# Rewriting the issue order of the last stage: TensorE's sequence written out, chunks of 2, 2, 4, 4, 4 and 2 tiles

## The chip, the cores and the metric

The kernel runs on one core of a Trainium2 chip. The time is the device time of one execution in microseconds (us). Three runs of the kernel before took 962.36, 962.38 and 963.45 us; their median is 962.38. About 0.2% (1.9 us) is what a measurement of this kernel can tell from no change.

## The reference, cut to what matters

Three layers follow each other. Attention through a small memory gives `x` (2304 tokens x 512). A mixture of eight experts sends each token to its best two. A last layer with a cosine gate gives the output:

```python
for e in range(E):                       # 8 experts, 512 -> 1024 -> 512
    for k in range(2):
        mask = top2[:, k] == e
        h = np.maximum(x[mask] @ w1[e], 0.0)
        out[mask] += top2_w[mask, k, None] * (h @ w2[e])
# last layer, on the experts' result
h = x @ w_in                             # 512 -> 2048
g = h * np.cos(h)
return (g @ w_out).astype(np.float32)    # 2048 -> 512
```

The change touches the seam between the last expert and the last layer, and the last layer itself.

## The kernel before, in words

Tokens are handled as 18 tiles of 128. Numbers that go through a matmul are split into two 16-bit parts, so each product is three matmuls: high by high, high by low, low by high.

**Experts.** Each expert has five second-layer tiles (`NST = 5`, capacity 640 rows). The first layer runs in two parts, over two of the tiles and then over the other three, in eight blocks each (`l1`, and `l1_out` on ScalarE and VectorE); the second layer runs tile by tile (`l2`, `l2_out`). `l2_out` scales on ScalarE and stores 128 rows to `yd` in memory. If an expert has more rows than 640, the loop `overflow` (L919) takes the rest; in these runs it has nothing to do, but its branch still joins all engines. Every matmul of the experts is tied to the one before by `chain("P", ...)`, which fixes TensorE's order.

**Last layer.** It works in chunks of tiles. `comb(t)` gathers a tile's two expert rows per token from `yd` (two indirect DMAs on POOL's queue), weights and adds them, finds a power-of-two scale in a chain of small VectorE instructions, splits the sum, and issues a transposing DMA into `x2T` on SP's queue. One small TensorE transpose (`pb`) and a ScalarE copy (`bct`) spread the scale over the columns. `m1(j, f)` computes block f of 16 of the first product for chunk j: 12 matmuls into one of four PSUM banks, four VectorE instructions (two of which read the bank, the second after a sine on ScalarE), a copy on ScalarE and a subtraction on POOL. Results lie in `gT`, in buffers that raw expert weights and the experts' hidden values used before. `m2_(t)` computes tile t's output: 48 matmuls, a scaled copy on ScalarE, a store.

**What sets the order.** Everything is entered in a list with a due time: `at(t, fn, ...)`. `issue()` sorts the list, and the due time becomes a priority; a scheduler then lays out each engine's queue from the priorities and its own estimate of when each instruction is ready. Only `chain` fixes an order. In the last layer before, nothing is chained, so the scheduler mixes first and second products on TensorE as it sees fit. Due times count from `X[e]`, the start of expert e, and `m0`, the end of the last expert. `put_weights` and `put_chunk` place loading, scaling and splitting of weights in free places (`slot`) on ScalarE and VectorE during the experts. In each engine, instructions run in queue order.

Of the kernel before, what the change touches and what calls it, by code (L numbers as in the profile page):

```python
# [60 lines left out]
def fused_kernel(ctx, tc, phiT, qT, kv, wgn, noise, w1, w2, wi, wo, out):  # L61
# [19 lines left out]
    def at(t, fn, *a, lead=None):  # L81
        line.append((t, len(line), fn, a, LEAD.get(fn.__name__, 0.0) if lead is None else lead))
# [18 lines left out]
    def l2k(shape, dt, name):  # L101
        return lp.tile(shape, dt, tag="l", name=name)
# [709 lines left out]
    def mt(shape, dt, name, bufs=2):  # L812
        return pools["mp"].tile(shape, dt, tag=name, name=name, bufs=bufs)
# [153 lines left out]

    ib = sm([P, NT], F32, "ib")
    x2T, bct = {}, {}
    chunks = [(0, 2), (2, 6), (6, 10), (10, 14), (14, 18)]  # L970
    ch_of = {t: j for j, (a, b) in enumerate(chunks) for t in range(a, b)}

    def comb(t):

        ys = []
        for k in range(2):
            y = l2k([P, DM], F32, f"y{k}")
            rows = min(YROWS, Y0 + (E - 1) * CAP + (t + 1) * P)
            G.indirect_dma_start(out=y, out_offset=None, in_=yd[0:rows],  # L979
                                 in_offset=bass.IndirectOffsetOnAxis(ap=sidx[:, t, k:k + 1], axis=0))  # L980
            ys.append(y)
        yield
        j = ch_of[t]
        o = (t - chunks[j][0]) * P
        if o == 0:
            n = (chunks[j][1] - chunks[j][0]) * P
            x2T[j] = mt([P, 8, n], F16, "x2T")
            bct[j] = mt([P, n], F32, "bct")
        y0, y1 = ys
        V.tensor_scalar(y0, y0, cw[:, t, 0:1], None, op0=OP.mult)  # L990
        V.scalar_tensor_tensor(y1, y1, cw[:, t, 1:2], y0, op0=OP.mult, op1=OP.add)  # L991
        mx = mt([P, 4], F32, "cmx")
        tmp = mt([P, 1], I32, "cmt")
        V.tensor_reduce(mx[:, 0:1], y1, axis=AX.X, op=OP.max, apply_absolute_value=True)
        pow2_scale(mx[:, 1:2], mx[:, 0:1], tmp)
        pow2_inv(ib[:, t:t + 1], mx[:, 1:2])
        V.tensor_scalar(mx[:, 2:3], ib[:, t:t + 1], 1.0 / (2.0 * math.pi), None, op0=OP.mult)
        hl = l2k([P, 2, DM], F16, "chl")
        A.activation(hl[:, 0], y1, AF.Copy, scale=mx[:, 1:2])
        V.scalar_tensor_tensor(hl[:, 1], y1, mx[:, 1:2], hl[:, 0], op0=OP.mult, op1=OP.subtract)  # L1000
        SP.dma_start_transpose(out=x2T[j][:, :, o:o + P], in_=hl.rearrange("p w d -> p (w d)"))
        yield
# [33 lines left out]
    def m1(j, f):  # L1036
        n = (chunks[j][1] - chunks[j][0]) * P
        if f % 8 == 0:
            gT[j, f // 8] = [hs("gT", int(2 * (f // 8) + w + j % 2 > 1), [P, 8, n], F16) for w in range(2)]
        ghi, glo = gT[j, f // 8]  # L1040
        x = x2T[j]
        c = f // 2
        w = win[c // 4][:, c % 4]
        fs = slice((f % 2) * P, (f % 2) * P + P)
        ph = bank_h()
        for k in range(4):
            T.matmul(ph[:, :n], lhsT=w[:, 0, k, fs], rhs=x[:, k, :], start=(k == 0), stop=False)  # L1047
            T.matmul(ph[:, :n], lhsT=w[:, 0, k, fs], rhs=x[:, 4 + k, :], start=False, stop=False)  # L1048
            T.matmul(ph[:, :n], lhsT=w[:, 1, k, fs], rhs=x[:, k, :], start=False, stop=(k == 3))  # L1049
        y = mt([P, 512], F32, "ty", 3)  # L1050
        t = mt([P, 512], F32, "tt", 3)
        V.scalar_tensor_tensor(y[:, :n], ph[:, :n], wis[:, 2 * E + c:2 * E + c + 1], bct[j], op0=OP.mult, op1=OP.mult)  # L1052
        V.tensor_scalar(t[:, :n], y[:, :n], 0.25, MAGIC, op0=OP.add, op1=OP.add)  # L1053
        V.scalar_tensor_tensor(t[:, :n], t[:, :n], MAGIC, y[:, :n], op0=OP.subtract, op1=OP.subtract)  # L1054
        A.activation(t[:, :n], t[:, :n], AF.Sin, bias=hp, scale=-2.0 * math.pi)  # L1055
        V.scalar_tensor_tensor(y[:, :n], ph[:, :n], fac[:, c:c + 1], t[:, :n], op0=OP.mult, op1=OP.mult)  # L1056
        A.activation(ghi[:, f % 8, :], y[:, :n], AF.Copy)  # L1057
        G.tensor_tensor(glo[:, f % 8, :], y[:, :n], ghi[:, f % 8, :], op=OP.subtract)  # L1058

    def m2_(t):  # L1060
        j = ch_of[t]
        cs = slice((t - chunks[j][0]) * P, (t - chunks[j][0] + 1) * P)
        po = bank_y()
        for f in range(16):
            ghi, glo = gT[j, f // 8]
            w = wout[f // 8][:, (f // 2) % 4]
            T.matmul(po, lhsT=ghi[:, f % 8, cs], rhs=w[:, 0, f % 2, :], start=(f == 0), stop=False)  # L1067
            T.matmul(po, lhsT=ghi[:, f % 8, cs], rhs=w[:, 1, f % 2, :], start=False, stop=False)  # L1068
            T.matmul(po, lhsT=glo[:, f % 8, cs], rhs=w[:, 0, f % 2, :], start=False, stop=(f == 15))  # L1069
        o = l2k([P, DM], F32, "o")  # L1070
# [48 lines left out]
    for e in range(E):  # L1119
        if e:  # L1120
            X.append(x)
            for f in range(8):
                x = put_l1(x, e, 0, f)
            if 0 < e < E - 1:
                at(x + 0.1, gather_x, e + 1, 0, False)
                for c in range(CA):
                    at(x + 4.0 + 0.5 * c, turn_x, e + 1, 0, c)
        for f in range(8):
            x = put_l1(x, e, 1, f)
        if e == 0:  # L1130
# [74 lines left out]
    x = X[7] + 8 * sum(d1)
    for t in range(6):
        y = x + d2 * (min(t, NST - 1) + 1) + 3.0 + (2.0 if t == 5 else 0.0)
        whole(y, comb, t)
    nj = len(chunks)
    x = m0  # L1210
    dm = lambda j: 16 * (1.4 if chunks[j][1] - chunks[j][0] == 2 else 2.64)

    def put_m1(j):
        nonlocal x
        for f in range(16):
            at(x + dm(j) / 16 * f, m1, j, f)
        x += dm(j)

    put_m1(0)
    for j in range(1, nj + 1):  # L1220
        if j < nj:
            put_m1(j)
        u0 = x
        for t in range(*chunks[j - 1]):
            at(x, m2_, t)
            x += 10.4
        if j + 1 < nj:
            per = (x - u0 - 2.0) / 4
            for k, t in enumerate(range(*chunks[j + 1])):
                y = u0 + per * k - 14.0  # L1230
                whole(y, comb, t)
    issue()


# [34 lines left out]
```

## Time and profile before

| | |
|---|---|
| median of three runs | 962.38 us |
| the profiled execution | 961.89 us |
| its span, first to last instruction | 960.1 us |
| mean granted TensorE clock | 0.964 |
| PE busy | 889.6 us (93%) |
| PEld (weight loads) busy | 496.9 us (52%) |
| DVE (VectorE) busy | 586.1 us (61%) |
| ACT (ScalarE) busy | 450.6 us (47%) |
| POOL (GpSimd) busy | 233.8 us (24%) |

A busy share is an average over stages with different limits. A wait is idle time of an engine just before an instruction, put down to what ended it. In the page's slices one digit stands for 24 us, in tenths busy. The last expert starts at about 504 us and the last layer fills the rest.

### The profile page before, as it was taken

What the parts mean: (1) busy time and instruction counts of PE and PEld (TensorE: products, weight loads), DVE (VectorE), ACT (ScalarE), POOL (GpSimd) and SP (SyncE); (2) the same over time, 40 slices, a digit from 0 to 9 for tenths busy, and PEclk for the clock granted to TensorE, in tenths of its full rate; (3) what the DMA queues carried; (4) which work ended last, traced back from release to release, by engine and by line L of the source; (5) the groups of instructions that cost most, each with busy time, mean ns of one, the idle gap of its engine ahead of it and who ended that gap; (6) DMA issues with size and microseconds to landing.
All of it is one profiled execution on the core that took longest, in us unless ns stands there. A gap on an engine that the chain in (4) does not pass through costs nothing. (4 is left out here: it accounts for less than half of the span.)

```text
span 960.1 us, 13569 instructions
## 1 busy us (share of the span) xinstructions
PE 889.6 (93%) x5124; PEld 496.9 (52%) x5124; DVE 586.1 (61%) x1290; ACT 450.6 (47%) x776; POOL 233.8 (24%) x228
## 2 busy tenths in 40 slices
PE   5988179999999999999999989599999999999998
PEld 3756055564747565655646456244444444444443
DVE  4799781375756567665855159599994695285000
ACT  3575603566666767666765125144552253143000
POOL 1354831111011102020100024344453243043000
PEclk9897679999999999999999989799999999999999
DMA  9962219768696879696780442522104102100000
GB/s 355 399 250 76 78 54 271 223 203 292 218 294 214 270 236 310 243 267 248 230 307 35 141 156 77 132 56 67 23 1 121 45 12 79 32 1 12 23 22 34
DMA packets 108244, 146.51 MB, mean 153 GB/s; under 512 B 65808, under 2 KB 66448, under 8 KB 106128
## 3 DMA queue, kind: packets, MB, share of 16 engines
q1 hardware_dynamic: 89536, 103.56, 34.4%
q0 software_dynamic: 6080, 19.93, 6.9%
q10 hardware_dynamic: 12560, 22.13, 6.3%
q8 instruction: 41, 0.67, 0.3%
q14 instruction: 27, 0.22, 0.1%
HBM read 95.26 MB, written 35.13 MB: 136 GB/s over the span
## 5 line engine op out<-in xcount | busy, mean ns | idle before, releaser
L244 PE MATMUL h<-x,w 128*128 128x384 f16 (+1 forms) x1440 | 201.2, 301 | 2.1 <-DVEq L924 2.1
L244 PEld LDWEIGHTS <-w 128*128 128x128 f16 x1440 | 140.9, 99 | 58.6 <-issue 2.8
L1058 POOL TENSOR_TENSOR gT<-ty,gT 128x512 f16<-128x512 f32 (+1 forms) x80 | 95.1, 1190 | 169.8 <-ACT gT L1057 169.8
L1047 PE MATMUL h<-x2T,win 128*128 128x512 f16 (+1 forms) x320 | 116.2, 363 | 8.7 <-DMA x2T<-chl 7.1
L907 PE MATMUL y<-w,hT 128*128 128x512 f16 x320 | 121.3, 379 | 0.0
L906 PE MATMUL y<-w,hT 128*128 128x512 f16 x320 | 121.3, 379 | 0.0
L905 PE MATMUL y<-w,hT 128*128 128x512 f16 x320 | 121.2, 379 | 0.0
L1048 PE MATMUL h<-x2T,win 128*128 128x512 f16 (+1 forms) x320 | 116.1, 363 | 0.0
L1049 PE MATMUL h<-x2T,win 128*128 128x512 f16 (+1 forms) x320 | 115.9, 362 | 0.0
L1067 PE MATMUL y<-wout,gT 128*128 128x512 f16 x288 | 108.8, 379 | 0.2 <-ACT gT L1057 0.2
L1068 PE MATMUL y<-wout,gT 128*128 128x512 f16 x288 | 108.8, 379 | 0.0
L1069 PE MATMUL y<-wout,gT 128*128 128x512 f16 x288 | 108.8, 379 | 0.0
L244 DVE SCALAR_TENSOR_TENSOR hT<-h,hT 128x384 f16<-128x384 f32 (+1 forms) x128 | 61.8, 488 | 72.7 <-ACT hT L244 71.2
L244 ACT ACTIVATE hT<-h 128x384 f16<-128x384 f32 (+1 forms) x128 | 55.8, 436 | 100.7 <-PE h L244 69.2
L244 DVE SCALAR_TENSOR_TENSOR w<-raw,wsc,w 128x1024 f16<-128x1024 f32 x56 | 71.2, 1282 | 26.2 <-ACT w L244 25.8
L1055 ACT ACTIVATE tt<-tt,hp 128x512 f32<-128x512 f32 (+1 forms) x80 | 54.3, 678 | 67.4 <-DVE tt L1054 61.5
L1052 DVE SCALAR_TENSOR_TENSOR ty<-h,wis,bct 128x512 f32<-128x512 f32 (+1 forms) x80 | 55.2, 690 | 45.9 <-PE h L1049 45.3
L1057 ACT ACTIVATE gT<-ty 128x512 f16<-128x512 f32 (+1 forms) x80 | 46.8, 587 | 69.3 <-DVE ty L1056 69.3
L844 POOL DMA_INDIRECT xg<-xd,idxB x24 | 25.8, 1076 | 216.3 <-DMA x<-xg 200.1
L244 ACT ACTIVATE w<-raw,wsc 128x1024 f16<-128x1024 f32 x56 | 62.8, 1139 | 3.8 <-ACT o L244 3.0
L979 POOL DMA_INDIRECT y<-yd,sidx x36 | 36.1, 1002 | 111.5 <-DMA yd<-o 89.6
L244 ACT ACTIVATE junk<-raw 128x1024 bf16<-128x1024 f32 x56 | 58.9, 1052 | 5.1 <-ACT o L244 4.7
(264 smaller groups left out, 1220.3 us busy)
## 6 DMA issues: line engine op xcount, KB each, us to landing
raw<-in_w SPq DMA_DIRECT2D x32, 1024.0 KB, 9.0
yd<-o ACTq DMA_DIRECT2D x40, 256.0 KB, 4.8
kvt<-in_kv SPq DMA_DIRECT2D x9, 1024.0 KB, 9.8
cvt<-in_wi SPq DMA_DIRECT2D x8, 1024.0 KB, 8.2
wst<-cvt SPq DMA_DIRECT2D x16, 512.0 KB, 3.7
cvt<-in_wo SPq DMA_DIRECT2D x8, 1024.0 KB, 6.2
yd<-zero ACTq DMA_DIRECT2D x13, 512.0 KB
xd<-hl SPq DMA_DIRECT2D x18, 256.0 KB, 2.6
```

Source lines behind the costliest of these rows:

```text
L244: last[key] = fn(*a, **kw)
L905: ins = [T.matmul(py, lhsT=hi[:, f, cs], rhs=w[:, 0, ws], start=(f == 0), stop=False), T.matmul(py, lhsT=hi[:, f, cs], rhs=w[:, 1, ws], st ...
L906: T.matmul(py, lhsT=hi[:, f, cs], rhs=w[:, 1, ws], start=False, stop=False),
L907: T.matmul(py, lhsT=lo[:, f, cs], rhs=w[:, 0, ws], start=False, stop=(f == 7))]
L1047: T.matmul(ph[:, :n], lhsT=w[:, 0, k, fs], rhs=x[:, k, :], start=(k == 0), stop=False)
L1048: T.matmul(ph[:, :n], lhsT=w[:, 0, k, fs], rhs=x[:, 4 + k, :], start=False, stop=False)
L1049: T.matmul(ph[:, :n], lhsT=w[:, 1, k, fs], rhs=x[:, k, :], start=False, stop=(k == 3))
L1052: V.scalar_tensor_tensor(y[:, :n], ph[:, :n], wis[:, 2 * E + c:2 * E + c + 1], bct[j], op0=OP.mult, op1=OP.mult)
L1058: G.tensor_tensor(glo[:, f % 8, :], y[:, :n], ghi[:, f % 8, :], op=OP.subtract)
L1067: T.matmul(po, lhsT=ghi[:, f % 8, cs], rhs=w[:, 0, f % 2, :], start=(f == 0), stop=False)
L1068: T.matmul(po, lhsT=ghi[:, f % 8, cs], rhs=w[:, 1, f % 2, :], start=False, stop=False)
L1069: T.matmul(po, lhsT=glo[:, f % 8, cs], rhs=w[:, 0, f % 2, :], start=False, stop=(f == 15))
```

## The change

Chunks become (2, 2, 4, 4, 4, 2) tiles instead of (2, 4, 4, 4, 4). Every matmul of the last layer and every `pb` transpose is tied into `chain("P", ...)`, so that TensorE runs them in the order of their due times. The last expert runs its first part's two second-layer tiles before its second part, and the first four blocks of chunk 0 before its last second-layer tile. From chunk 2 on, second products of one chunk stand between groups of the next chunk's first products. `comb` loses its steps: its first multiply goes to ScalarE, the output scale `osc` is computed there instead of in `m2_`, the scale buffers become four, and the `pb` transpose becomes a function of its own, `c_bct`, with its own due time. The due times of the overflow loop, the pools, the table load, the output weights and the last expert's second weights move.

```diff
-    chunks = [(0, 2), (2, 6), (6, 10), (10, 14), (14, 18)]
+    chunks = [(0, 2), (2, 4), (4, 8), (8, 12), (12, 16), (16, 18)]
...
-        V.tensor_scalar(y0, y0, cw[:, t, 0:1], None, op0=OP.mult)
+        A.activation(y0, y0, AF.Copy, scale=cw[:, t, 0:1])
...
-        mx = mt([P, 4], F32, "cmx")
+        mx = mt([P, 4], F32, "cmx", 4)
...
+        V.tensor_tensor(osc[:, t:t + 1], ib[:, t:t + 1], ik, op=OP.mult)
...
+    def c_bct(t):
+        j, o = c_place(t)
         pb = mbank("pb")
-        T.transpose(pb[:, :P], mx[:, 2:3].to_broadcast([P, P]), ident)
-        A.activation(bct[j][:, o:o + P], pb[:, :P], AF.Copy)
-        yield
+        chain("P", T.transpose, pb[:, :P], cm.pop(t)[:, 2:3].to_broadcast([P, P]), ident)
+        A.activation(bct[j][:, o], pb[:, :P], AF.Copy)
...
-            T.matmul(ph[:, :n], lhsT=w[:, 0, k, fs], rhs=x[:, k, :], start=(k == 0), stop=False)
+            chain("P", T.matmul, ph[:, :n], lhsT=w[:, 0, k, fs], rhs=x[:, k, :], start=(k == 0), stop=False)
...
-            T.matmul(po, lhsT=ghi[:, f % 8, cs], rhs=w[:, 0, f % 2, :], start=(f == 0), stop=False)
+            chain("P", T.matmul, po, lhsT=ghi[:, f % 8, cs], rhs=w[:, 0, f % 2, :], start=(f == 0), stop=False)
...
+        if e == E - 1:
+            for c in range(CA):
+                x = put_l2(x, e, c)
         for f in range(8):
             x = put_l1(x, e, 1, f)
+        if e == E - 1:
+            break
...
+    def put_comb(t, t0, t1):
+        at(t0, comb, t)
+        at(t1, c_bct, t)
+
+    y = [ends[-8 - CA + t] for t in range(2)]
+    put_l2_ = lambda c: put_l2(x, E - 1, c)
+    x = put_l2_(2)
+    x = put_l2_(3)
+    for t in range(2):
+        put_comb(t, y[t] + 3.0, x - 2.0 + t)
+    put_m1(0, range(0, 4))
+    x = put_l2_(4)
     m0 = x
+    put_m1(0, range(4, 16))
+    put_m2(0)
+    put_comb(2, m0 + 3.0, x)
+    put_m2(1)
+    put_comb(3, m0 + 6.0, x - 1.0)
+    put_m1(1, range(16))
+    put_m2(2)
+    for t in range(4, 8):
+        put_comb(t, m0 + 9.0 + 9.0 * (t - 4), x + (0.0 if t < 7 else 9.0))
+    put_m2(3)
+    put_m1(2, range(16))
+    for j, first, u in ((2, 2, 24.0), (3, 0, 58.0), (4, 2, 40.0)):
+        n = chunks[j + 1][1] - chunks[j + 1][0]
+        u0, u1 = x - u, x + first * 10.36
+        for k, t in enumerate(range(*chunks[j + 1])):
+            put_comb(t, u0 + (u1 - u0 - 16.0) / n * k, u1 - 0.2 * n + 0.1 * k)
+        for k in range(4):
+            if k >= first:
+                q = 16 // (4 - first)
+                put_m1(j + 1, range(q * (k - first), q * (k - first + 1)))
+            put_m2(chunks[j][0] + k)
+    for t in range(*chunks[5]):
+        put_m2(t)
...
-    OV, LP, PRE = 22.0, 34.0, 36.0
+    OV, LP, PRE = 13.0, 16.0, 30.0
+    x = X[E - 2]
+    put_weights(2 * E - 1, (x + 12.0, x + 15.0), x + 27.0, 0.0)
...
-        put_chunk(c, X[1] + 2.0 + 19.3 * c)
+        put_chunk(c, X[1] + 2.0 + 18.5 * c)
...
-    at(X[7] + 37.0, load_wout, 0)
-    at(m0 + 0.5, load_wout, 1)
+    at(X[7] + 45.0, load_wout, 0)
+    at(m0 + 4.0, load_wout, 1)
```

`put_m1(j, fs)` places the blocks `fs` of chunk j at 1.31 us (two tiles) or 2.59 us (four), `put_m2(t)` a second product at 10.36 us.

## Rows read from the trace of the kernel before

**Rows 1.** The page's slices: PE's busy tenths in 40 slices of 24 us.
```profile
PE   5988179999999999999999989599999999999998
```
**Rows 2.** PE's waits from 480 us: who, for what: us in total, times, longest.
```profile
PE h L1047 <- DMA x2T<-chl: 7.1, 2, 4.6
PE pb L1004 <- DVE osc L1071: 5.6, 1, 5.6
PE pb L1004 <- ACT bct L1005: 2.2, 1, 2.2
PE h L244 <- DVEq L924: 2.1, 1, 2.1
```
**Rows 3.** Stretches: length, busy us of PE, PEld, DVE, ACT, POOL, clock, DMA.
```profile
560.00:570.00 10.00, 6.73 (x42) 5.11 (x43) 2.92 (x9) 1.40 (x5) 1.89 (x2) 0.66 0.95 308
...
566.40:598.80 32.40, 32.33 (x237) 23.39 (x236) 29.51 (x80) 15.26 (x35) 12.38 (x17) 0.98 0.31 98
```
**Rows 4.** PE in order of time: start, us, instruction, idle time before it.
```profile
503.63 0.27 PE L244 MATMUL h<-x,w 128*128 128x256 f16 x1
...
558.23 0.27 PE L1004 MATMUL pb<-ident,cmx 128*128 128x128 f32 x1
560.71 0.34 PE L1004 MATMUL pb<-ident,cmx 128*128 128x128 f32 x1 [2.20 <-ACT bct L1005]
...
569.42 0.27 PE L1049 MATMUL h<-x2T,win 128*128 128x256 f16 x1
...
571.28 0.27 PE L1048 MATMUL h<-x2T,win 128*128 128x256 f16 x1
...
831.45 0.38 PE L1047 MATMUL h<-x2T,win 128*128 128x512 f16 x1
...
841.81 0.38 PE L1067 MATMUL y<-wout,gT 128*128 128x512 f16 x1
```
**Rows 5.** ACT in order of time.
```profile
560.38 0.28 ACT L1005 ACTIVATE bct<-pb 128x128 f32<-128x128 f32 x1 [0.41 <-ACT o L244]
561.08 0.28 ACT L1005 ACTIVATE bct<-pb 128x128 f32<-128x128 f32 x1 [0.43 <-PE pb L1004]
...
567.76 0.51 ACT L1055 ACTIVATE tt<-tt,hp 128x256 f32<-128x256 f32 x1 [6.40 <-DVE tt L1054]
...
738.46 0.27 ACT L1005 ACTIVATE bct<-pb 128x128 f32<-128x128 f32 x1
...
945.62 0.69 ACT L1072 ACTIVATE o<-y,osc 128x512 f32<-128x512 f32 x1 [9.67 <-PE y L1069]
...
955.98 0.69 ACT L1072 ACTIVATE o<-y,osc 128x512 f32<-128x512 f32 x1 [9.67 <-PE y L1069]
```
**Rows 6.** DVE's groups by shape, 566 to 876 us: busy, mean ns, idle before.
```profile
L1056 DVE SCALAR_TENSOR_TENSOR ty<-h,fac,tt 128x256 f32<-128x256 f32 x16 | 7.6, 475 | 0.8 <-ACT tt L1055 0.8
L1052 DVE SCALAR_TENSOR_TENSOR ty<-h,wis,bct 128x256 f32<-128x256 f32 x16 | 7.6, 474 | 7.0 <-PE h L1049 7.0
L1054 DVE SCALAR_TENSOR_TENSOR tt<-tt,ty 128x256 f32<-128x256 f32 x16 | 7.4, 460 | 0.1
L1053 DVE TENSOR_SCALAR tt<-ty 128x256 f32<-128x256 f32 x16 | 6.2, 388 | 0.2
```
**Rows 7.** DVE in order of time, in a run of 512-column blocks.
```profile
683.37 0.75 DVE L1056 SCALAR_TENSOR_TENSOR ty<-h,fac,tt 128x512 f32<-128x512 f32 x1 [0.19 <-ACT tt L1055]
...
686.03 0.75 DVE L1056 SCALAR_TENSOR_TENSOR ty<-h,fac,tt 128x512 f32<-128x512 f32 x1 [0.19 <-ACT tt L1055]
```
**Rows 8.** DVE in order of time: tile 0's combine, and a lone L1053.
```profile
545.93 0.75 DVE L991 SCALAR_TENSOR_TENSOR y<-y,cw,y 128x512 f32<-128x512 f32 x1 [0.99 <-DMA y<-yd,sidx]
...
548.76 0.75 DVE L1000 SCALAR_TENSOR_TENSOR chl<-y,cmx,chl 128x512 f16<-128x512 f32 x1 [0.34 <-ACT chl L999]
...
566.97 0.29 DVE L1053 TENSOR_SCALAR tt<-ty 128x256 f32<-128x256 f32 x1
```
**Rows 9.** The gathers of the last layer, 540 to 830 us.
```profile
DMA to landing us min/median/max: 3.3/4.3/7.3
```

More of the change, by code (lines that the diff above doesn't have):

```diff
@@ L969, in fused_kernel, with c_place @@
     x2T, bct = {}, {}
-    chunks = [(0, 2), (2, 6), (6, 10), (10, 14), (14, 18)]
+    chunks = [(0, 2), (2, 4), (4, 8), (8, 12), (12, 16), (16, 18)]
     ch_of = {t: j for j, (a, b) in enumerate(chunks) for t in range(a, b)}
+    cm = {}
+    def c_place(t):
+        j = ch_of[t]
+        return j, slice((t - chunks[j][0]) * P, (t - chunks[j][0] + 1) * P)
     def comb(t):
[L975 to L978, printed above, removed]
+        rows = min(YROWS, Y0 + (E - 1) * CAP + (t + 1) * P)
+        y0, y1 = (l2k([P, DM], F32, f"y{k}") for k in range(2))
+        for k, y in enumerate((y0, y1)):
             G.indirect_dma_start(out=y, out_offset=None, in_=yd[0:rows],
                                  in_offset=bass.IndirectOffsetOnAxis(ap=sidx[:, t, k:k + 1], axis=0))
-            ys.append(y)
-        yield
-        j = ch_of[t]
-        o = (t - chunks[j][0]) * P
-        if o == 0:
+        j, o = c_place(t)
+        if t == chunks[j][0]:
             n = (chunks[j][1] - chunks[j][0]) * P
@@ L988, in comb @@
             bct[j] = mt([P, n], F32, "bct")
-        y0, y1 = ys
-        V.tensor_scalar(y0, y0, cw[:, t, 0:1], None, op0=OP.mult)
+        A.activation(y0, y0, AF.Copy, scale=cw[:, t, 0:1])
         V.scalar_tensor_tensor(y1, y1, cw[:, t, 1:2], y0, op0=OP.mult, op1=OP.add)
-        mx = mt([P, 4], F32, "cmx")
+        mx = mt([P, 4], F32, "cmx", 4)
         tmp = mt([P, 1], I32, "cmt")
@@ L1000, in comb @@
         V.scalar_tensor_tensor(hl[:, 1], y1, mx[:, 1:2], hl[:, 0], op0=OP.mult, op1=OP.subtract)
-        SP.dma_start_transpose(out=x2T[j][:, :, o:o + P], in_=hl.rearrange("p w d -> p (w d)"))
-        yield
+        SP.dma_start_transpose(out=x2T[j][:, :, o], in_=hl.rearrange("p w d -> p (w d)"))
+        cm[t] = mx
+    def c_bct(t):
+        j, o = c_place(t)
         pb = mbank("pb")
-        T.transpose(pb[:, :P], mx[:, 2:3].to_broadcast([P, P]), ident)
-        A.activation(bct[j][:, o:o + P], pb[:, :P], AF.Copy)
-        yield
+        chain("P", T.transpose, pb[:, :P], cm.pop(t)[:, 2:3].to_broadcast([P, P]), ident)
+        A.activation(bct[j][:, o], pb[:, :P], AF.Copy)
     win, wout = [], []
@@ L1038, in m1 @@
         if f % 8 == 0:
-            gT[j, f // 8] = [hs("gT", int(2 * (f // 8) + w + j % 2 > 1), [P, 8, n], F16) for w in range(2)]
-        ghi, glo = gT[j, f // 8]
+            gT[j, f // 8] = [hs("gT", int(j % 2 == 0 or 2 * (f // 8) + w == 3), [P, 8, n], F16) for w in range(2)]
         x = x2T[j]
@@ L1046, in m1 @@
         for k in range(4):
-            T.matmul(ph[:, :n], lhsT=w[:, 0, k, fs], rhs=x[:, k, :], start=(k == 0), stop=False)
[L1048 to L1058, printed above, removed]
+            chain("P", T.matmul, ph[:, :n], lhsT=w[:, 0, k, fs], rhs=x[:, k, :], start=(k == 0), stop=False)
+            chain("P", T.matmul, ph[:, :n], lhsT=w[:, 0, k, fs], rhs=x[:, 4 + k, :], start=False, stop=False)
+            chain("P", T.matmul, ph[:, :n], lhsT=w[:, 1, k, fs], rhs=x[:, k, :], start=False, stop=(k == 3))
+        y = mt([P, 512], F32, "ty", 3)[:, :n]
+        t = mt([P, 512], F32, "tt", 3)[:, :n]
+        ghi, glo = gT[j, f // 8]
+        V.scalar_tensor_tensor(y, ph[:, :n], wis[:, 2 * E + c:2 * E + c + 1], bct[j], op0=OP.mult, op1=OP.mult)
+        V.tensor_scalar(t, y, 0.25, MAGIC, op0=OP.add, op1=OP.add)
+        V.scalar_tensor_tensor(t, t, MAGIC, y, op0=OP.subtract, op1=OP.subtract)
+        A.activation(t, t, AF.Sin, bias=hp, scale=-2.0 * math.pi)
+        V.scalar_tensor_tensor(y, ph[:, :n], fac[:, c:c + 1], t, op0=OP.mult, op1=OP.mult)
+        A.activation(ghi[:, f % 8, :], y, AF.Copy)
+        G.tensor_tensor(glo[:, f % 8, :], y, ghi[:, f % 8, :], op=OP.subtract)
     def m2_(t):
-        j = ch_of[t]
-        cs = slice((t - chunks[j][0]) * P, (t - chunks[j][0] + 1) * P)
+        j, cs = c_place(t)
         po = bank_y()
@@ L1066, in m2_ @@
             w = wout[f // 8][:, (f // 2) % 4]
-            T.matmul(po, lhsT=ghi[:, f % 8, cs], rhs=w[:, 0, f % 2, :], start=(f == 0), stop=False)
-            T.matmul(po, lhsT=ghi[:, f % 8, cs], rhs=w[:, 1, f % 2, :], start=False, stop=False)
-            T.matmul(po, lhsT=glo[:, f % 8, cs], rhs=w[:, 0, f % 2, :], start=False, stop=(f == 15))
+            chain("P", T.matmul, po, lhsT=ghi[:, f % 8, cs], rhs=w[:, 0, f % 2, :], start=(f == 0), stop=False)
+            chain("P", T.matmul, po, lhsT=ghi[:, f % 8, cs], rhs=w[:, 1, f % 2, :], start=False, stop=False)
+            chain("P", T.matmul, po, lhsT=glo[:, f % 8, cs], rhs=w[:, 0, f % 2, :], start=False, stop=(f == 15))
         o = l2k([P, DM], F32, "o")
-        V.tensor_tensor(osc[:, t:t + 1], ib[:, t:t + 1], ik, op=OP.mult)
         A.activation(o, po, AF.Copy, scale=osc[:, t:t + 1])
@@ L1103, in put_l1 @@
         ends.append(x)
-        if part or f % 2:
+        if part or f % 4:
             free.append(x + 0.05)
@@ L1137, in fused_kernel, with put_m1, put_m2 @@
             x = put_l2(x, e, c)
-    m0 = x
+    def put_m1(j, fs):
+        nonlocal x
+        n = chunks[j][1] - chunks[j][0]
+        d = 1.31 if n == 2 else 2.59
+        for f in fs:
+            at(x, m1, j, f)
+            x += d
+    def put_m2(t):
+        nonlocal x
+        at(x, m2_, t)
+        x += 10.36
+    def put_comb(t, t0, t1):
[9 more added lines that the diff above has]
+    x = put_l2_(4)
+    m0 = x
+    put_m1(0, range(4, 16))
[21 more added lines that the diff above has]
+        put_m2(t)
     def next_table():
@@ L1192, in fused_kernel @@
         put_weights(2 * e, (x - 6.0, x - 3.0), x + 11.5, 0.0)
-        put_weights(2 * e + 1, (x + 15.0, x + 18.0), x + 30.0, 0.0)
+        if e < E - 1:
+            put_weights(2 * e + 1, (x + 12.0, x + 15.0), x + 30.0, 0.0)
     bg(slots(), X[1] + 8.0, (0, 6, 12, 18))
@@ L1200, in fused_kernel @@
     at(X[7] + 0.3, load_win, 1)
-    at(m0 - 1.0, factors)
+    at(X[7] + 17.0, factors)
     at(X[7] + PRE, next_table)
-    at(X[7] + 37.0, load_wout, 0)
-    at(m0 + 0.5, load_wout, 1)
[L1205 to L1231, printed above, removed]
+    at(X[7] + 45.0, load_wout, 0)
+    at(m0 + 4.0, load_wout, 1)
     issue()
```

## The prediction

> **What bounds the kernel now.** I read the page's slices first. PE is at nine tenths or more in nearly every slice from the fifth on, except in a hole in slices 23 to 25, where the last expert gives way to the last stage [rows 1]. So outside that hole time can come only from fewer matmuls, and the change removes none. Second, PE's own waits from 480 us on: 7.1 us for a transposed tile, 5.6 us for VectorE's scale of a combined tile, 2.2 us for ScalarE to empty the bank of the small transposes (the pb matmuls), 2.1 us at the branch of the overflow loop; behind these four there is little [rows 2]. Third, the stretches: the granted clock is 0.66 from 560 to 570 us, so the matmuls behind such a hole run partly at the lower level, and from 566.4 to 598.8 us VectorE is busy 29.5 of 32.4 us while PE loses nothing [rows 3]. There PE alternates between first and second products: the second products fill the time in which VectorE is behind.
>
> **How much is at stake.** The last expert's first matmul starts at 503.63 us and the last output copy, which follows PE's end directly, at 955.98 [rows 4, 5]: 452.35 us. The floor of the new order, with the same matmuls:
> - last expert, with the branch: 558.23 - 503.63 = 54.6 [rows 4].
> - first products: 17 matmuls of 256 columns from 569.42 to 571.28, 0.1094 each, so a chunk of two tiles (16 blocks f of 12) costs 21.0; 48 of 512 columns from 831.45 to 841.81, 10.36, so a chunk of four costs 41.44 [rows 4]. Three of each: 187.3. (Trading a chunk of four for two of two adds 0.6.)
> - second products: 10.36 a tile by the distance of the last two output copies [rows 5], 18 tiles: 186.5.
> - 18 pb transposes. Their rows show 0.27 for one, which is pipelined; I take 0.11, that of a 256-column matmul: 2.0.
>
> Sum 430.4, so 22.0 us of holes, slow clock and small waits lie in before's last stage. The branch is not among them: it moves to another place but still joins all engines, and stays at 2.1.
>
> **What the fixed order removes.** With two second-layer tiles of the last expert done early, tile 1's rows are complete at about 23 us after the expert's start (10.5 + 2 x 5.2 + 2.1), and the first products begin at about 49. From the row that starts VectorE's combine to its end takes 3.6 us [rows 8] and a gather 3.3 to 7.3 us to land [rows 9]; even with a store and a transpose of like length that is under 26. So the transfer wait at 563 goes. The one at 619 goes too: tiles 2 and 3 now have at least 36 us of matmuls behind the last expert (12 blocks and two second products), tiles 4 to 7 some 78. I count all 22.0 as removed.
>
> **What it adds, first: pb transposes back to back.** They now stand in PE's order in groups of 2, 1, 1, 3, 1, 4, 4 and 2, and use one PSUM bank. Each later one of a group waits until ScalarE has copied the one before. By the pair in the trace: pb at 560.71, its copy at 561.08 for 0.28, and a copy that ended at 560.66 let the next pb start at 560.71: 0.37 + 0.28 + 0.05 = 0.70 a turn, 0.6 over its own 0.11 [rows 4, 5]. All five groups stand right behind a finished output tile, whose copy (0.69) is ahead on ScalarE; the row at 738.46 shows a bct copy starting without idle time behind such work [rows 5]. So the first turn costs 1.0. Two groups of four 2 x (1.0 + 0.6 + 0.6), one of three 1.6, two pairs 2.0: 8.0 us. Before, PE ran other matmuls there. Low end: the copy goes ahead of the output tile, 10 x 0.6 = 6.0. High end: the output's DMA issue goes first as well, the 0.41 that stands in the row at 560.38, five times: 10.0.
>
> **Second: narrow chunks with nothing between their blocks.** A block f needs four VectorE instructions. Their means at 256 columns are 0.474, 0.388, 0.460 and 0.475 [rows 6]; less about 0.075 by which dense rows overlap, 1.50 a block, against PE's 1.31. High end: the whole stretch of rows 3, 80 VectorE instructions, some 16 blocks and two combines, gives (32.4 - 2 x 2.7)/16 = 1.69. Low end: no slower than PE. A combine keeps VectorE for 1.5 (its two instructions of 0.75 alone) to 3.2 us (from 545.93 to 549.51 less 0.34 idle [rows 8]); I take 2.7, nearer the whole, as the small instructions between cost time too and other blocks fill only part of their gaps. The change moves its first multiply to ScalarE, which is left out here. PE may be four banks ahead: 4 x 1.31, less the block's own 1.31 and its unhurried chain to the second read of the bank, 0.48 + 0.79 (566.97 to 567.76) + 0.51 + 0.03 + 0.48 = 2.3 [rows 5, 8]: 1.64 us of slack.
> - Chunk 0, blocks 4 to 15 (0 to 3 are covered by the last second-layer tile): 12 x 1.50 + 1.5 combines x 2.7 = 22.05 against 15.75 + 1.64: 4.65 us.
> - Chunk 1: 16 x 1.50 + one combine 2.7 = 26.7 against 21.0 + 1.64: 4.05 us. Tile 6 waits for tile 2's pb (four scale buffers), tile 7 for tile 3's, so one of them falls in here.
> - Chunk 5 is cut in halves by a second product: 8 x 1.50 = 12.0 against 10.5 + 1.64: nothing.
> - At 512 columns VectorE's period in steady state is 686.03 - 683.37 = 2.66, of which 0.19 is idle [rows 7], against PE's 2.59 with four times that as lead. Over 16 blocks it falls behind by 1.1, plus two combines, and catches up in the second products: nothing.
>
> Sum 8.7.
>
> **Costed at nothing.** The last expert's second weights are due earlier in the written plan: their last piece at 6.5 us before the expert's start instead of 15.6 after it, needed at 10.5 after; the first weights' last piece comes at 2.5 before, read from 1.2 after. ScalarE and VectorE do the same work there, and PE has no wait from that part [rows 2]; if the cover went, each late piece would cost 1 to 2 us. On SP's queue both loads of the output weights start later; the second has 16.9 us from its due time to its first use, more than twice the slowest gather [rows 9]. The table load lands among the last expert's relus, where PE is four banks ahead. The early stores wait for nothing new. Scales moved from the output to the combine stay on VectorE.
>
> **Sum.** -22.0 + 8.0 + 8.7 = -5.3 us. The profiled execution took 961.89 us, 0.49 below the median of 962.38; carried over to the median: 957.1 us.
>
> **Rivals.**
> - *The order is as free as it was meant*: bct copies go first (6.0) and VectorE keeps up with 1.31. -22.0 + 6.0 = -16.0: 946.4 us. For it: part of the stretch's 29.5 us was combines, which now fall into second products. Against it: 1.50 is a mean of all sixteen blocks.
> - *VectorE is the bound of the narrow chunks*, and PE, whose order is fixed, has nothing to put in between. At 1.7 a block and 3.2 a combine: chunk 0 20.4 + 4.8 - 17.4 = 7.8; chunk 1 27.2 + 3.2 - 22.6 = 7.8; chunk 5 2 x (13.6 - 12.1) = 2.9 (rounded). With 8.0 for the pb turns: +4.5, 966.9 us. It decides from 1.63 a block on, where these stalls reach 14.0. For it: the high end above, and L1053's mean of 0.388 against 0.29 for a lone one [rows 6, 8], beside POOL's subtractions. Against it: that stretch also had more combines.
>   The Trainium skill (page "SBUF — State Buffer", section "Who interferes with whom") says that a VectorE instruction with two SBUF inputs, or in a two-port mode, and a GpSimd instruction that reads SBUF shut each other out for a whole instruction; by that rule the narrow blocks, which bring a subtraction every 1.31 us, fare as in this rival. L1053's 0.1 us of excess agrees in sign, and is far less than a whole subtraction.
> - *Late gathers*: VectorE works in order; if a gather in chunk 0 lands after 7.3 instead of 3.3 us [rows 9], because the second load of weights runs beside it, blocks behind the combine wait 4.0 longer: -1.3, 961.1 us.
> - *The order isn't what it says*: PE's order would still alternate first and second products inside a chunk, and nothing would change. The links are written instruction by instruction, so this is small and counted with the third.
>
> **How the numbers follow.** Forecast 0.42, free order 0.20, VectorE-bound 0.23, late gathers 0.15. 0.2% of 962 is 1.9 us, about what a measurement of this kernel tells from no change. Faster: nearly all of the forecast and the free order, and a little of the third, 0.62. Same: most of the third, 0.14. Slower: VectorE-bound and its neighbours, 0.24. Range: from 947, the free order, to 968, just past the VectorE-bound case. The forecast's own range, from the ends of the pb and VectorE terms short of the rivals, is 952 to 961.
>
> **What would show it.** In the changed profile: no PE wait on a transposed tile; five places with PE waits on ACT bct of 1.0 and 0.6, in all 6 to 10; PE waits in chunks 0 and 1, 4 to 5 in each, on VectorE's second read of the bank (L1056 of before); clock 1.0 from 560 to 625. It is wrong if PE waits on a gather or a scale again, if the wait at the branch grows, or if the narrow chunks run through at 1.31 a block.

## The result: slower, and the profile after

| kernel | median us (runs) | ratio to before, 95% | last stage us |
|---|---|---|---|
| before | 962.4 (959.3 to 963.5, 4) | 1 | 452.3 |
| changed | 976.4 (973.6 to 977.6, 4) | 1.0147 [1.0115, 1.0179] | 465.5 |
| changed, PE's order free (e1) | 943.5 (942.3 to 944.9, 4) | 0.9802 [0.9778, 0.9827] | 433.2 |

Each ratio is to runs of the kernel before taken beside it. The forecast was 957.1 us, faster, and the range ended at 968. "Last stage" is, here and below, the time from the last expert's first matmul to PE's end in the profiled execution, the stretch that the prediction summed up (452.35 to the output copy, floor 430.4). In the changed kernel it runs from 504.13 to 969.67 us: 13.2 us longer than before, 35.1 over the floor.

The page's slices of the changed kernel, PE and the granted clock. Counted from 0, as the prediction does, PE's old hole in slices 23 to 25 [rows 1] has become shallower, and slices 28 and 32 have new dents:

```profile
PE   5988179999999999999999989799799989999998
...
PEclk8988579999999999999999999999999999999999
```

PE's waits in its last stage (from 500 us):

```profile
PE h L244 <- DVE ty L1061: 17.2, 13, 3.8
PE pb L244 <- ACT bct L1010: 6.0, 10, 0.8
PE y L907 <- issue: 2.1, 1, 2.1
PE h L244 <- DVE ib L158: 1.7, 2, 1.2
```

The waits for a transposed tile and for a combine's scale [rows 2] are gone. In their place stand the ten pb turns and thirteen waits for VectorE's second read of a bank (L1061, which is L1056 of before; two more are put down to L158, the instruction right behind an L1061). Where these are, by stretches (length, busy us of PE, PEld, DVE, ACT, POOL, clock, DMA): blocks 4 to 15 of chunk 0, chunk 1, the sixteen blocks of chunk 2, and for comparison four blocks of chunk 4:

```profile
565.10:584.10 19.00, 16.39 (x146) 14.08 (x145) 17.12 (x44) 9.79 (x21) 9.41 (x12) 1.00 0.51 172
605.10:635.00 29.90, 23.38 (x195) 19.67 (x194) 25.90 (x73) 15.04 (x33) 11.32 (x14) 0.94 0.27 55
657.80:710.90 53.10, 45.53 (x194) 19.50 (x192) 48.85 (x93) 23.42 (x36) 23.49 (x19) 0.94 0.23 55
...
822.40:832.80 10.40, 10.40 (x50) 4.71 (x49) 6.60 (x11) 3.39 (x5) 1.50 (x2) 1.00 0.07 26
```

At the floor's rates these stretches take 15.75, 21.0 and 41.44 us. So chunk 0 loses 3.2, chunk 1 8.8 and chunk 2 11.7 us; chunk 3 loses 1.0 and 1.5 in its two halves, chunk 5 0.2. With 8.2 for the pb turns that is 34.6 of the 35.1.

A group of four pb transposes in PE's timeline (start, us, instruction, idle before). The next first product starts 2.70 us after the first pb, where four pb on their own would take 0.44, at the 0.11 from the lone pb at 594.58 to the matmul behind it at 594.69:

```profile
731.65 0.27 PE L244 MATMUL pb<-ident,cmx 128*128 128x128 f32 x1
732.76 0.32 PE L244 MATMUL pb<-ident,cmx 128*128 128x128 f32 x1 [0.84 <-ACT bct L1010]
733.45 0.32 PE L244 MATMUL pb<-ident,cmx 128*128 128x128 f32 x1 [0.37 <-ACT bct L1010]
734.14 0.32 PE L244 MATMUL pb<-ident,cmx 128*128 128x128 f32 x1 [0.37 <-ACT bct L1010]
734.35 1.02 PE L244 MATMUL h<-x2T,win 128*128 128x512 f16 x4
```

VectorE's groups in chunk 2 (first four lines) and in chunk 4 (last line): busy, mean ns of one, idle before. Four combines lie inside chunk 2's run (x4), and L1059 takes half as long again as in chunk 4:

```profile
L1059 DVE SCALAR_TENSOR_TENSOR tt<-tt,ty 128x512 f32<-128x512 f32 x14 | 14.1, 1008 | 0.0
...
L1061 DVE SCALAR_TENSOR_TENSOR ty<-h,fac,tt 128x512 f32<-128x512 f32 x13 | 9.6, 735 | 0.0
...
L1002 DVE SCALAR_TENSOR_TENSOR chl<-y,cmx,chl 128x512 f16<-128x512 f32 x4 | 4.5, 1131 | 0.0
...
L999 DVE TENSOR_TENSOR osc<-ib,ik 128x1 f32<-128x1 f32 x4 | 1.7, 413 | 0.0
...
L1059 DVE SCALAR_TENSOR_TENSOR tt<-tt,ty 128x512 f32<-128x512 f32 x10 | 6.9, 690 | 0.2
```

### The profile page after: what moved, and what is told of

The parts are those of the page before. It is cut to its first block, busy times and chain, and to the rows that moved or that the text cites. A ratio compares the mean times of both kernels' runs of the same rounds, so it can differ in the third digit from the quotient of the medians.

```text
span 973.8 us, 14080 instructions
## 1 busy us (share of the span) xinstructions
PE 896.3 (92%) x5316; PEld 515.9 (53%) x5316; DVE 590.9 (61%) x1336; ACT 468.8 (48%) x826; POOL 235.2 (24%) x244
## 5 line engine op out<-in xcount | busy, mean ns | idle before, releaser
L244 PE MATMUL h<-x2T,win 128*128 128x256 f16 (+1 forms) x1152 | 196.9, 331 | 19.2 <-DVE ty L1061 17.2
L244 PE MATMUL y<-wout,gT 128*128 128x512 f16 x864 | 188.7, 379 | 0.0
L244 PEld LDWEIGHTS <-win 128*128 128x128 f16 x1152 | 114.2, 99 | 99.9 <-issue 27.4
L1063 POOL TENSOR_TENSOR gT<-ty,gT 128x256 f16<-128x256 f32 (+1 forms) x96 | 99.0, 1036 | 264.4 <-ACT gT L1062 264.3
L244 PEld LDWEIGHTS <-gT 128*128 128x128 f16 x864 | 84.5, 98 | 101.2 <-POOL gT L1063 0.7
L1057 DVE SCALAR_TENSOR_TENSOR ty<-h,wis,bct 128x256 f32<-128x256 f32 (+1 forms) x96 | 58.4, 610 | 114.9 <-PE h L244 112.5
L1060 ACT ACTIVATE tt<-tt,hp 128x256 f32<-128x256 f32 (+1 forms) x96 | 58.9, 614 | 79.7 <-DVE tt L1059 69.2
L1062 ACT ACTIVATE gT<-ty 128x256 f16<-128x256 f32 (+1 forms) x96 | 49.9, 521 | 70.6 <-DVE ty L1061 70.1
L1061 DVE SCALAR_TENSOR_TENSOR ty<-h,fac,tt 128x256 f32<-128x256 f32 (+1 forms) x96 | 58.4, 608 | 7.7 <-ACT tt L1060 7.7
L1059 DVE SCALAR_TENSOR_TENSOR tt<-tt,ty 128x256 f32<-128x256 f32 (+1 forms) x96 | 60.8, 634 | 0.7
```

Source lines behind the costliest of these rows:

```text
L244: last[key] = fn(*a, **kw)
L1057: V.scalar_tensor_tensor(y, ph[:, :n], wis[:, 2 * E + c:2 * E + c + 1], bct[j], op0=OP.mult, op1=OP.mult)
L1059: V.scalar_tensor_tensor(t, t, MAGIC, y, op0=OP.subtract, op1=OP.subtract)
L1060: A.activation(t, t, AF.Sin, bias=hp, scale=-2.0 * math.pi)
L1061: V.scalar_tensor_tensor(y, ph[:, :n], fac[:, c:c + 1], t, op0=OP.mult, op1=OP.mult)
L1062: A.activation(ghi[:, f % 8, :], y, AF.Copy)
```

## The experiments

The planner sorts PE's matmuls when the kernel is built, by its own estimates and the due times; on the chip PE always works in order. "Free" below means sorted by the planner, "fixed" written out.

**e1: PE's order free.** `chain("P", ...)` taken off the last stage's products and pb:

```diff
-            chain("P", T.matmul, ph[:, :n], lhsT=w[:, 0, k, fs], rhs=x[:, k, :], start=(k == 0), stop=False)
+            T.matmul(ph[:, :n], lhsT=w[:, 0, k, fs], rhs=x[:, k, :], start=(k == 0), stop=False)
```

> The changed kernel with the last layer's matmuls and pb transposes not tied to each other, so the scheduler orders TensorE as before the change; chunks, early tiles, due times and combine stay. Theory A (the fixed order leaves TensorE nothing to put in while VectorE is behind): the 26 us of waits in chunks 0 to 3 and the 8 us of pb turns are mostly filled again, and the early tiles still save the hole at the seam: 950 to 962 us. Rival C (the other edits are what costs): it stays above 970 us.

Measured: 943.5 us, below A's 950 to 962; last stage 433.2, 2.8 over the floor. No other line differs from the changed kernel (but the planner lays out the other engines' queues anew), so the written order costs 33 us and the rest of the change gains 19. PE's longest waits from 500 us, its timeline in chunk 2, and the whole of chunk 2's run as a stretch:

```profile
PE h L1050 <- DVE ty L1061: 2.5, 3, 1.7
...
```

```profile
678.56 0.38 PE L1072 MATMUL y<-wout,gT 128*128 128x512 f16 x1
678.77 0.38 PE L1050 MATMUL h<-x2T,win 128*128 128x512 f16 x1
...
681.15 0.38 PE L1052 MATMUL h<-x2T,win 128*128 128x512 f16 x1
681.37 0.38 PE L1073 MATMUL y<-wout,gT 128*128 128x512 f16 x1
```

```profile
642.20:692.50 50.30, 48.03 (x223) 21.61 (x222) 45.35 (x90) 23.24 (x35) 21.30 (x18) 1.00 0.26 66
```

The sixteen blocks take 50.3 us here, against 53.1, and VectorE is busy 45.4 us in them, against 48.9: it is hardly faster. But PE puts second products of the same chunk between them, from blocks that are already finished, and so the time is not lost.

**e2: chunk 2 cut in halves by a second product.**

```diff
-        put_comb(t, m0 + 9.0 + 9.0 * (t - 4), x + (0.0 if t < 7 else 9.0))
+        put_comb(t, m0 + 9.0 + 9.0 * (t - 4), x)
+    put_m1(2, range(8))
     put_m2(3)
-    put_m1(2, range(16))
+    put_m1(2, range(8, 16))
```

> One move in the fixed order: tile 3's second product stands between blocks 0-7 and 8-15 of chunk 2 instead of ahead of all sixteen. Theory A: in chunk 2 (53.1 us for 41.4 us of matmuls in the changed kernel) the 11.7 us of loss fall to 3 to 5, because VectorE gets 10.4 us more inside the run; 967 to 970 us. Rival B (VectorE loses its time to POOL's subtractions, block by block, whatever stands between): the loss stays at 9 or more, 974 us or more.

Measured: 971.3 us, ratio 1.0086 [1.0055, 1.0117]. The first half (646.77 to 667.49) ran at 20.72 us without loss, the second (677.85 to 700.16) lost 1.6. VectorE began two combines in the whole run, both in the second half:

```profile
682.56 0.75 DVE L992 SCALAR_TENSOR_TENSOR y<-y,cw,y 128x512 f32<-128x512 f32 x1
...
692.77 1.19 DVE L992 SCALAR_TENSOR_TENSOR y<-y,cw,y 128x512 f32<-128x512 f32 x1 [1.34 <-ACT gT L1062]
```

So the edit did two things: it cut the run, and it left two combines in it in place of four. The two second products behind the run then took 26.1 us in place of 20.7: the first waited 3.2 us for its operand (gT), with a stretch at half clock behind the wait. Tile 7's pb came into the back-to-back group (0.7). In all 7.7 in place of 11.7, and the medians differ by 5.1: the direction fits A, the size fell short, as A had no price for the wait on gT.

**e3: chunk 3's tiles combined without VectorE.**

```diff
+        if 8 <= t < 12:
+            V.memset(mx, 1.0)
+            A.activation(hl[:, 0], y0, AF.Copy)
+            A.activation(hl[:, 1], y1, AF.Copy)
...
+            return
```

> Tiles 8 to 11 are combined without VectorE: their weighting, scale and split are left out (two ScalarE copies and a constant instead), the gathers, transposes and pb stay. Theory A (four combines fall into chunk 2's run): chunk 2's loss of 11.7 falls to at most 2; about 966 us. Rival B (POOL's subtractions slow VectorE's blocks): the excess of L1059 in chunk 2 (1.02 us mean against 0.69 in chunk 4) stays and 5 us or more remain, 970 us or more.

Measured: 964.4 us, ratio 1.0019 [1.0002, 1.0036]. Chunk 2 as a stretch:

```profile
656.10:697.60 41.50, 41.50 (x195) 18.83 (x194) 36.46 (x57) 25.58 (x41) 19.75 (x17) 1.00 0.24 58
```

The run is at its floor, with POOL's subtractions still there: without combines VectorE keeps up at 512 columns. The excess that B wanted to see stay is gone from L1059 (0.69 us in the mean here), while L1058 took 0.61 in place of 0.42; VectorE could bear that.

**e4: chunk 2's subtraction on POOL replaced by a memset.**

```diff
-        G.tensor_tensor(glo[:, f % 8, :], y, ghi[:, f % 8, :], op=OP.subtract)
+        if j == 2:
+            G.memset(glo[:, f % 8, :], 0.0)
```

> In chunk 2 POOL writes zeros into the low part instead of subtracting (the low part of chunk 2 is left out); VectorE's work and all orders stay. Rival B: L1059 in chunk 2 falls from 1.02 to about 0.7 us and the loss of 11.7 to 3 or less: 965 to 968 us. Theory A in its plain form (too many VectorE instructions in the run, collisions or not): the loss stays at 7 or more, 972 us or more.

Measured: 968.1 us, ratio 1.0050 [1.0025, 1.0075], at the upper end of B's numbers. Chunk 2 as a stretch, and its L1059:

```profile
657.00:702.20 45.20, 41.97 (x194) 18.77 (x193) 42.13 (x85) 22.79 (x36) 9.67 (x14) 1.00 0.24 53
```

```profile
L1059 DVE SCALAR_TENSOR_TENSOR tt<-tt,ty 128x512 f32<-128x512 f32 x14 | 9.4, 678 | 0.0
```

The zeros were not written block by block but in two bursts of eight, one ahead of the run and one early in it. POOL's second burst, and the VectorE instruction beside it:

```profile
663.22 3.80 POOL L1064 MEMSET gT<- 128x512 f16 x8
```

```profile
664.29 3.01 DVE L1058 TENSOR_SCALAR tt<-ty 128x512 f32<-128x512 f32 x1
```

That one instruction takes 0.42 us elsewhere in the run. Chunk 2 loses 3.8 in place of 11.7, this included, with three combines in it and the first part of the fourth. So neither alone makes the loss: the combines put VectorE behind, and POOL's subtractions make combines and blocks longer.

**e5: only the pb transposes free**, the products still fixed.

```diff
-        chain("P", T.transpose, pb[:, :P], cm.pop(t)[:, 2:3].to_broadcast([P, P]), ident)
+        T.transpose(pb[:, :P], cm.pop(t)[:, 2:3].to_broadcast([P, P]), ident)
```

> The changed kernel, but the 18 small transposes (pb) are no links of PE's fixed order; all other matmuls of the last stage still are. In the changed kernel ten pb turns in five groups cost 8.2 us of PE's time. Theory A (fixed order has nothing between the pb turns, and nothing between the first products while VectorE is behind; the two add up): about 968, 8 us below the changed kernel, and no PE wait on ScalarE's bct copy. Rival D (the pb turns are hidden, because behind them PE would wait for VectorE anyway): 974 to 977.

Measured: 968.5 us, ratio 1.0065 [1.0043, 1.0087]. The pb waits are gone, those on VectorE stay:

```profile
PE h L244 <- DVE ty L1061: 18.0, 12, 3.7
...
PE h L244 <- DVE ib L158: 1.6, 2, 1.2
```

**e6: fixed, but finer.** Pieces of three matmuls of the chunk before stand behind each block:

```diff
+    def put_mix(j, us):
+        for f in range(16):
+            put_m1(j, range(f, f + 1))
+            put_m2(us[len(us) * f // 16:len(us) * (f + 1) // 16])
```

> PE's order is still fixed to the last instruction, but finer: a second product is cut into 16 pieces of three matmuls, and pieces of the chunk before stand behind each block of first products of chunks 1 to 5; each pb transpose stands behind two such pieces or more. Chunks, early tiles and the work of the other engines as in the changed kernel. Theory A (the cost is that of unbroken runs and of back-to-back turns, not of fixing): of the 35 us lost over the floor 8.2 (pb) and some 23 (chunks 1 to 3) go, chunk 0 keeps its 3: 945 to 952. Rival F (a fixed order costs whatever its grain, because PE waits in order for whatever engine is late): 960 or more.

Measured: 962.4 us, ratio 1.0008 [0.9998, 1.0018], last stage 455.1. It missed A's number, and F's came in: 14 of the 31 us that A wanted came back. PE's waits from 500 us:

```profile
PE h L244 <- DVE ty L1061: 9.1, 8, 2.3
PE pb L244 <- ACT bct L1010: 6.5, 4, 4.0
```

An even spread is no cure. The longest wait on VectorE, 2.3 us, ends at 684.90: at 683.44 VectorE had started a combine's first instruction (L992) after standing 2.44 us for its gathered rows. And a pb in the written order waited 4.0 us for ScalarE's copy of the pb before it; that copy stood behind a combine's multiply (L991), which was waiting for its rows too.

**e7 and e8: what makes the 19 us.** Each is e1 with one part as before: e7 the last expert's first two output tiles late, e8 chunks of 2, 4, 4, 4, 4 with due times to fit.

```diff
-        if e == E - 1:
-            for c in range(CA):
-                x = put_l2(x, e, c)
```

```diff
-    chunks = [(0, 2), (2, 4), (4, 8), (8, 12), (12, 16), (16, 18)]
+    chunks = [(0, 2), (2, 6), (6, 10), (10, 14), (14, 18)]
```

> The free-order version (943.5 us: the changed kernel with no fixed order in the last stage), but the last expert's first two output tiles come after all its first-layer blocks, as in the kernel before. If the early tiles are what removes the holes (waits for a transposed tile 7.1, for a scale 5.6 us, and the low clock behind them, in the kernel before): 949 to 956, with PE waiting for a transposed tile again. If the rest of the change (six chunks, combines due earlier, the multiply on ScalarE) removes them: 943 to 946.

> The free-order version (943.5 us), but with the chunks of the kernel before (2,4,4,4,4 tiles); early tiles, ScalarE's multiply and free order stay. If the chunk of two behind the first is needed, because four tiles must be combined before the next chunk can start: PE waits for a scale or a transposed tile, 947 to 953. If the early tiles alone do it: 942 to 945 (the narrow chunks' extra 0.6 us is saved).

Measured: e7 954.8 us, 0.9919 [0.9898, 0.9941]; e8 953.8 us, 0.9913 [0.9893, 0.9933], 0.8 above the range expected. PE's waits of e7, then of e8:

```profile
PE h L1050 <- DVE ty L1061: 4.9, 5, 1.5
PE pb L1009 <- ACT bct L1010: 4.0, 1, 4.0
...
PE h L1050 <- DMA x2T<-chl: 1.8, 1, 1.8
```

```profile
PE h L1050 <- DMA x2T<-chl: 5.0, 1, 5.0
PE pb L1009 <- DVE osc L999: 3.5, 1, 3.5
```

Each part without the other keeps some 8 us of the gain, both together 19. The early tiles empty the seam before chunk 0, the chunk of two the one before chunk 1.

**e9, e11, e12: e1's order, written out.** e9 copied it from e1's trace in blocks and in groups of three, one tile after the other. e11 copied it matmul by matmul, with the two tiles that are open at a time; e12 also gave the combines e1's due times. In the order of e11, h5.12 is all twelve matmuls of block 5, y0.2 the next two of tile 0's second product.

```diff
+    ORDER = ("h0.12 h1.12 h2.12 h3.12 h4.12 y0.2 y1.2 y0.1 y1.1 h5.12 y0.3 h6.12 h7.12 y0.5 h8.12 "
...
+    for tok in ORDER.split():
```

> PE's order is fixed again, but to the order that the free version (943.5 us) was seen to run in, copied from its trace in whole blocks of twelve first-product matmuls and groups of three second-product matmuls: a second product starts on the finished blocks of its own chunk, and a chunk's first two to five blocks stand ahead of its last pb transposes. Theory A (what costs is which matmuls stand next to each other, not that the order is fixed): 943 to 949. Rival F (a fixed order costs by itself, whatever stands in it): 955 or more.

> PE's order is fixed matmul by matmul to the order in which the free version (943.5 us) was built, two open second products and all: between its first products stand second products of the same chunk, of two tiles in turn, behind the blocks that they need, and not, as in the block-wise copy (1002.8 us), one tile's pieces right behind the block that they read. Theory A (it matters only what stands next to what; fixing an order costs nothing by itself): 942 to 947. Rival F (fixing costs by itself): 955 or more.

> As the matmul-wise copy (949.4 us), but each combine is due when it is in the free version; in the copy before, the combine of tile 4 and of later tiles was due later, and PE, in its fixed order, waited 3.7 us for the scale of tile 4 at its pb transpose. If that wait was made by the due time (theory A): it goes, with the low clock behind it, 942 to 946. If a fixed order costs by itself (rival F): 948 to 950 again, with a wait of like length at another place.

Measured: e9 1002.8 us, 1.0433 [1.0416, 1.0450]; e11 949.4 us, 0.9857 [0.9836, 0.9878]; e12 949.7 us, 0.9865 [0.9848, 0.9881]. PE's waits of e9, e11 and e12:

```profile
PE y L244 <- ACT gT L1070: 29.3, 19, 3.0
```

```profile
PE pb L244 <- DVE osc L999: 3.7, 1, 3.7
PE h L244 <- DVE ty L1069: 3.1, 3, 1.6
```

```profile
PE h L244 <- DVE ty L1069: 8.6, 3, 6.3
```

e9 came out where F had it, but it was no copy: with one tile at a time a piece stood right behind the block that it reads, and waited for it nineteen times. In the traces of e11 and e12 first products, second products and pb follow each other in the same order as in e1's, matmul by matmul. These two take back 27 of the 33 us with a fixed order, so fixing by itself is not the price of those; but both missed A's number by 2 to 4 us. In e12 rival F's value came in, and the trace shows where the last 6 us come from. ScalarE and VectorE in order of time, e12:

```profile
605.52 0.72 ACT L991 ACTIVATE y<-y,cw 128x512 f32<-128x512 f32 x1 [7.00 <-DMA y<-yd,sidx]
```

```profile
606.28 0.75 DVE L992 SCALAR_TENSOR_TENSOR y<-y,cw,y 128x512 f32<-128x512 f32 x1 [6.96 <-ACT y L991]
...
608.46 0.48 DVE L1065 SCALAR_TENSOR_TENSOR ty<-h,wis,bct 128x256 f32<-128x256 f32 x1
```

and VectorE at the same place in e1:

```profile
601.32 0.48 DVE L1057 SCALAR_TENSOR_TENSOR ty<-h,wis,bct 128x256 f32<-128x256 f32 x1 [6.33 <-PE h L1052]
...
602.05 0.74 DVE L992 SCALAR_TENSOR_TENSOR y<-y,cw,y 128x512 f32<-128x512 f32 x1
```

In e12 a combine whose multiply on ScalarE waits for its gathered rows stands in VectorE's own order ahead of chunk 1's first block; in e1 the block goes first. With PE's order the same, the orders of the other engines differ, and PE waits 6.3 us for it. A version with all engines' orders copied was not tried.

**e10: e1 with the combine's first multiplication on VectorE.**

```diff
-        A.activation(y0, y0, AF.Copy, scale=cw[:, t, 0:1])
+        V.tensor_scalar(y0, y0, cw[:, t, 0:1], None, op0=OP.mult)
```

> The free-order version (943.5 us) with the combine's first multiplication back on VectorE, as in the kernel before. If a free order covers VectorE: 943 to 945. If VectorE's load still sets the end somewhere in the free version: 946 or more (18 instructions of 512 columns more on VectorE).

Measured: 944.4 us, 0.9823 [0.9807, 0.9840], which can't be told from e1. In a free order that multiplication's engine decides nothing.

## Why the prediction was wrong

- **The holes removed, -22.0: right.** PE waits on no transposed tile and no combine's scale at a seam; chunk 0 starts at once behind its pb turn. e1 shows it best: with nothing added, the stage is 433.2 for a floor of 430.4, 19 of the 22 gained.
- **The pb turns, +8.0: right.** 8.2 us in five groups; freeing them alone gave 7.9 (976.4 to 968.5).
- **The branch, unchanged: right** (2.1 us).
- **VectorE behind the first products, +8.7: the step that failed; it is 26.4.** Its sentence "At 512 columns ... plus two combines, and catches up in the second products: nothing" cost most: chunk 2 lost 11.7 and chunk 3 2.5. Two terms of it were off:
  - *The count of combines.* Not two but four combines lie in chunk 2's run. The diff says so: with x the end of that run the four are due at x - 24, x - 16.8, x - 9.6 and x - 2.5.
  - *PE's lead.* It was taken as four whole blocks, 10.36, where the prediction's own lead at 256 columns leaves out a block's own time and its chain to the second read; worked out that way it is some 4.4 (4 x 2.59 less the block's own 2.59 and its chain of some 3.35 at 512 columns).

  Four combines with the old lead would give 1.6, two with the new one 2.1, both together 16 x 2.66 + 4 x 2.7 = 53.4 against 41.4 + 4.4: 7.5. PE's fixed order has nothing to put in there, and e3 takes the whole loss away by taking just these combines off VectorE.

  Chunk 3's halves, with two combines each, come to 1.6 each by the same terms; 1.0 and 1.5 were measured. In chunk 1 two combines fell, not one (L992 at 609.63 and 619.05), and the second waited 1.3 us for its rows: 4.05 + 2.7 + 1.3 = 8.05, where 8.8 were measured. Chunk 0 had one in place of 1.5: 3.3 by the same terms, 3.2 measured. So the count of combines in each run and the lead at 512 columns were wrong.

  That the prices of a block and of a combine then fit is in part luck: where POOL had no subtractions (e4) they are too high, as chunk 2 lost 3.8 and not 7.5 there, and in the changed kernel they stand in for POOL's share, of which L1059's excess alone, 16 x (1.01 - 0.68), is 5.3.
- **What no step held: the clock.** Three times PE idled 2.1 to 3.8 us in such a run, and then worked at half clock (below); 1.7 us in chunk 1 and 3.2 in chunk 2. With them chunk 2 adds up to 10.7 of its 11.7, but chunk 1 to 9.75, more than its 8.8: the terms are no better than 1 us. The sign "clock 1.0 from 560 to 625" failed at its end: from 623.4 us the clock was 0.50.
- **What only a rival held: POOL.** The rival "VectorE is the bound" had mechanism and sign right and the place wrong: it charged the narrow chunks 18.5, where 12.2 were lost, and the wide ones nothing, where 14.2 were. e4 shows POOL's part in it: some 7.9 of chunk 2's 11.7, the 3.2 of half clock included. The figure is rough, as part of the fourth combine fell behind the run there.
- **The free-order rival** (946.4) was thought of as a quick VectorE. VectorE isn't quick; e1 gets below its time by covering it.
- **Late gathers**: in the changed kernel seen once, 1.3 us in chunk 1, not the 4.0 in chunk 0. In other fixed orders that rival's mechanism did come in: 2.44 us on VectorE in e6, 7.00 on ScalarE in e12, with PE's longest waits on VectorE (2.3 and 6.3) behind them.

## What to carry to other kernels

Before an order is written out, count for each unbroken run what else the engine that drains it has due in that time, from the due times themselves: here four combines in 41 us, with subtractions beside them, were the difference between nothing and 12 us. A planned order that mixes two kinds of work covers such bursts. Where an order is fixed, the other engines' orders have to fit it: one misfit cost 6.3 us in e12. That fixing them all takes this back was not shown. Judge the parts of a change apart: this one held 19 us of gain under 33 us of loss.

## What the runs showed of the hardware

**VectorE and POOL shut each other out.** The changed kernel, VectorE and then POOL in order of time:

```profile
681.79 1.22 DVE L999 TENSOR_TENSOR osc<-ib,ik 128x1 f32<-128x1 f32 x1
...
684.04 1.53 DVE L1059 SCALAR_TENSOR_TENSOR tt<-tt,ty 128x512 f32<-128x512 f32 x1
```

```profile
681.82 3.21 POOL L1063 TENSOR_TENSOR gT<-ty,gT 128x512 f16<-128x512 f32 x2
```

L999 multiplies one column and took 1.22 us beside POOL's subtraction, 0.14 or 0.15 in 15 of the 18 combines. L1059's mean was 1.01 us in chunk 2 and 0.68 where POOL had no subtractions (e4). L1061, one of whose inputs is the bank, kept 0.74 in both. POOL's subtractions took 1.49 us in the mean in chunk 2, and 1.26 where no combines stood beside them (e3). The Trainium skill (page "SBUF — State Buffer", section "Who interferes with whom") says that a VectorE instruction with two SBUF inputs contends with a GpSimd instruction that reads SBUF, and not with one that only writes it. Both rows agree on the reading, and the one-column instruction shows a wait of 1.1 us, nearly a whole subtraction, where the prediction had seen an excess of 0.1 in L1053. What the page says of writing no run here shows: no L1059 stood beside e4's zeros, and the L1058 that did, which has one large input, took 3.01 us.

**A short wait can cost a second time.** Stretches of the changed kernel around the resumption of work after PE's waits of 3.75, 2.78 and 2.07 us; the first line holds the wait of 3.75 itself and what stands ahead of it (the number ahead of the DMA share is the granted clock):

```profile
610.00:623.30 13.30, 8.47 (x77) 7.29 (x75) 11.90 (x36) 6.00 (x14) 6.58 (x8) 1.00 0.33 60
623.40:626.70 3.30, 3.30 (x18) 2.32 (x17) 3.27 (x12) 1.48 (x3) 1.39 (x2) 0.50 0.00 0
688.30:691.60 3.30, 3.00 (x8) 1.08 (x8) 3.30 (x7) 1.35 (x2) 2.16 (x2) 0.50 0.00 0
705.30:708.60 3.30, 3.30 (x10) 1.18 (x8) 3.30 (x6) 1.23 (x2) 2.17 (x2) 0.50 0.00 0
```

```profile
688.60 4.23 PE L244 MATMUL h<-x2T,win 128*128 128x512 f16 x12 [2.78 <-DVE ty L1061]
...
699.24 2.75 PE L244 MATMUL h<-x2T,win 128*128 128x512 f16 x12 [0.78 <-DVE ty L1061]
```

At 0.5, the lower level of 1.2 GHz, twelve 512-column matmuls took 4.23 us in place of 2.75. In chunk 0, with waits of 0.94, 0.44 and 1.18 us, the row above shows 1.00. Nor does one length of wait decide it: behind the same 2.1 us at the branch the clock was 1.00 in the changed kernel (522.4 to 525.9 us) and 0.53 in e11 (520.0 to 523.4).
